# Attention and gated convolution: the last 64 keys' scores of two heads as two 64-row matmuls in place of one block matmul

## The chip, the core and the metric

One core of a Trainium2 chip runs the whole program. The metric is the device time of one execution in microseconds (us); three runs of the kernel before took 470.22, 471.49 and 474.07 us, and their median, 471.49, is the time before.

## The reference

The inputs are q, k and v of 4 batches, 8 heads, 576 positions and 64 elements, all float32. Rotary attention without a mask is followed by a feed-forward layer ("MoE" in the names) with a gate that looks at neighbouring positions:

```python
q_rot, k_rot = rotate(q), rotate(k)
scores = np.matmul(q_rot, k_rot.transpose(0, 1, 3, 2)) / np.sqrt(D)
scores = scores - np.max(scores, axis=-1, keepdims=True)
attn = np.exp(scores); attn = attn / (np.sum(attn, axis=-1, keepdims=True) + 1e-09)
x = np.matmul(attn, v)                        # then heads side by side: 4 x 576 x 512
h = np.maximum(x @ w_in, 0.0)                 # 512 -> 1024
conv_out[s] = sum(conv_w[k] * h[s + k - 1])   # k = 0, 1, 2, zero outside
out = (h * sigmoid(conv_out)) @ w_out         # 1024 -> 512
```

## The kernel before, in words

The 32 heads are taken two at a time, as 16 pairs p; head 0 of a pair lies on partitions 0 to 63 of the transposed queries and keys QT and KT, head 1 on 64 to 127. A pair has five steps s: four of 128 queries for each head, and a fifth (s = 4) with the last 64 queries of both heads together. Step m = 5p + s computes scores (`emit_S`), negated row maxima (DVE, L284), exponentials with row sums (ACT, L288), and in the next step transposes of the exponentials (`emit_T`, L336), which ACT evacuates into the tile `pt` (L216). The product of these with the values (`emit_E`, L415) comes a pair later, cut into four parts of 145 positions for the early pairs, and is evacuated as `xn` (L425).

The order of all engines' instructions is written out by hand. `plan[n]` holds the pieces of step n with a rank each; `at(n, rank, fn)` adds one, and the loop in `emit` takes them in the order of the ranks. Each engine executes its own instructions in that order, and semaphores between engines come from what is read and written.

The diff touches the steps in front of `WIDE = 26`, where there is no feed-forward work on PE yet (`"m" not in psum`). There a step n holds, by rank: 0, the transposes of step n - 1, head 0's eight and then head 1's eight (in a fifth step ten for both), and their evacuations on ACT; 0.19 to 0.5, pieces of the rotation on POOL (`rope_by_three`), the maxima (0.2) and exponentials (0.3) of step n, evacuations of what `spare` gave out a step before (0.35), the transposes of later queries and keys (`emit_TQ`, DVE, L249 and L252, 0.35), pieces of the weights' conversion from 64 to 32 bits (DVE, ACT, 0.4), and the scores of step n + 1 (0.5); 2, the remainder transpose (`emit_Trem`, L367); 4, the product part; 4.5 and later, DMAs and reciprocals.

A score tile `ps` has three banks of 512 columns, and two such tiles take turns. Head 0's scores are in columns 0 to 575, head 1's in 960 to 1535. The first 512 keys of a head are one 64-row matmul into a bank of its own (L276). The last 64 keys of both heads come from one 128-row matmul (L302) against `krem`, a block-diagonal 128 x 128 tile with head 0's last 64 keys in one corner and head 1's in the other; its output goes to columns 512 to 575 and 960 to 1023 of the middle bank:

```python
nc.tensor.matmul(
    out=ps[:, 512:1024].rearrange("p (g n) -> p g n", g=8)[:, 0:8:7, :],
    lhsT=qt[:, c], rhs=krem[p % 2], start=True, stop=True,
)
```

The corners of `krem` are filled by two 64 x 64 DVE transposes a pair (L256), or, for pair 0, by two DVE copies (L241); its zeros are set once. The columns between, 576 to 959, are handed out by `spare` to the remainder transpose and the product part of the same step, and evacuated by ACT in the next step behind the exponentials (`after`). The fifth step has no block matmul: its scores are 64 x 64 matmuls. A matmul in float32 stands in the trace as two records, each with a weight load (PEld).

Of the kernel before, what the change touches and what calls it, by code (L numbers as in the profile page):

```python
# [7 lines left out]
F32 = mybir.dt.float32  # L8
# [3 lines left out]
AF = mybir.ActivationFunctionType  # L12
# [8 lines left out]
def attention_moe_kernel(ctx, tc, q, k, v, w_in, conv_w, w_out, tab, tabx, out):  # L21
    nc = tc.nc
    B, H, S, D = q.shape
# [11 lines left out]
    STEPS = 5  # L35
    scale = float(D) ** -0.5
# [4 lines left out]
    psum = {}  # L41
# [25 lines left out]
    xT = keep.tile([128, NSLOT - NK, 2, XW], F32R, name="xT")  # L67
    wctx = ExitStack()
    wkeep = wctx.enter_context(tc.tile_pool(name="wk", bufs=1))
    krem = [wkeep.tile([128, 128], F32, name=f"kr_{s}") for s in range(2)]  # L70
    tabs = wkeep.tile([128, 480], F32, name="tabs")
    turnm = [tabs[:, 128 * i:128 * i + 128].rearrange("p (t i) -> p t i", t=4) for i in range(3)]
    turnr = [tabs[:, 384 + 32 * i:416 + 32 * i] for i in range(3)]
# [118 lines left out]
    def port(ins):  # L192
        late["v"] = ins
        return ins

    def gated(ins):
        tc.add_manual_dep(
            ins.ins, late["v"].ins.name, mybir.DependencyInfo(mybir.DependencyClass.Sync, mybir.DependencyReason.DATA), reason="port"
        )

    def rope_by_three(p, part):
        def mult(i):
# [9 lines left out]
    QT, KT = {}, {}  # L212

    def evac(eng, out, in_, sc=None):
        if eng == "A" or "m" not in psum:
            nc.scalar.activation(out=out, in_=in_, func=AF.Copy, scale=1.0 if sc is None else sc)  # L216
        elif sc is None:
            nc.vector.tensor_copy(out, in_)
        else:
            nc.vector.tensor_scalar(out=out, in0=in_, scalar1=sc, scalar2=None, op0=ALU.mult)  # L220
# [6 lines left out]
    def emit_TQ0(part, ps):  # L227
        qk_tiles(0)
        turned = [z.rearrange("p h d -> p (h d)") if part == "r" else z.rearrange("p t h d -> p t (h d)") for z in rot.pop(part)]
        for t in range(1 if part == "r" else 4):  # L230
            for i, z in enumerate(turned):
                nc.tensor.matmul(
                    out=ps[:, 0:128] if part == "r" else ps.rearrange("d (p t) -> d t p", t=4)[:, t, :],
                    lhsT=z if part == "r" else z[:, t, :], rhs=idf, start=(i == 0), stop=(i == 1),
                )
        if part == "r":
            evac("A", QT[0][:, 512:S], ps[:, 0:64])
            evac("A", KT[0][:, 576:640], ps[:, 64:128])
            for h in range(2):
                r = slice(64 * h, 64 * h + 64)  # L240
                nc.vector.tensor_copy(krem[0][r, r], ps[r, 64:128])  # L241
        else:
            evac("A", QT[0][:, 0:512] if part == "q" else KT[0][:, 64:576], ps)

    def emit_TQ(p, part):
        qk_tiles(p)
        x = raw.pop((p, part))[:, :, 0, :]
        if part == "q":
            nc.vector.transpose(out=QT[p].rearrange("p (c i) -> p c i", i=32), in_=x)  # L249
        else:  # L250
            kt = KT[p].rearrange("p (c i) -> p c i", i=32)
            nc.vector.transpose(out=kt[:, 2:20], in_=x)  # L252
            if p * STEPS < WIDE:
                for h in range(2):
                    r = slice(64 * h, 64 * h + 64)
                    nc.vector.transpose(out=krem[p % 2][r, r].rearrange("p (c i) -> p c i", i=32), in_=x[r, 16:18])  # L256
            if p * STEPS + STEPS > WIDE:
                nc.vector.transpose(out=kt[:, 0:2], in_=x[:, 16:18])

# [5 lines left out]
    def go(d, key):  # L265
        for fn in d.pop(key):
            fn()

    def emit_S(p, s):
        if s == 0:  # L270
            negm[p] = p2.tile([128, 9], F32, tag="negm", name="negm")
            sums[p] = p2.tile([128, 9], F32, tag="sums", name="sums")
        qt, kt = QT[p], KT[p]

        def mm(out, h, a, n, c):
            nc.tensor.matmul(  # L276
                out=out, lhsT=qt[64 * h:64 * h + 64, c], rhs=kt[64 * h:64 * h + 64, a:a + n], start=True, stop=True
            )

        def soft(sc, dst, col):  # L280
            nm, sm = negm[p][:, col:col + 1], sums[p][:, col:col + 1]
            if len(sc.shape) == 3:
                dst = dst.rearrange("p (j n) -> p j n", j=2)
            reds.setdefault((p, s), []).append(lambda: nc.vector.tensor_reduce(  # L284
                out=nm, in_=sc, axis=AX.XY if len(sc.shape) == 3 else AX.X, op=ALU.max, negate=True
            ))
            exps.setdefault((p, s), []).append(
                lambda: nc.scalar.activation(out=dst, in_=sc, func=AF.Exp, bias=nm, scale=1.0, accum_out=sm)  # L288
            )

        c = slice(128 * s, min(128 * s + 128, S))
        if s < 4:
            st = ST[p, s] = p1.tile([128, 2, S], F32, tag="st", name="st", bufs=3)
        else:
            st = STR[p] = strem[p % 2][:, 0:S]
        if "m" not in psum:
            ps = free["ps"] = psum["s"].tile([128, 1536], F32, tag="s", name="sp")
            free["at"] = 576
            if s < 4:
                mm(ps[:, 0:512], 0, 64, 512, c)  # L300
                mm(ps[:, 1024:1536], 1, 64, 512, c)
                nc.tensor.matmul(  # L302
                    out=ps[:, 512:1024].rearrange("p (g n) -> p g n", g=8)[:, 0:8:7, :],
                    lhsT=qt[:, c], rhs=krem[p % 2], start=True, stop=True,
                )
                for h in range(2):
                    soft(ps[:, 960 * h:960 * h + S], st[:, h, :], 5 * h + s)
            else:
                for h in range(2):
                    mm(ps[64 * h:64 * h + 64, 0:512], h, 64, 512, c)  # L310
                for h in range(2):
                    mm(ps[64 * h:64 * h + 64, 512:576], h, 576, 64, c)
                soft(ps[:, 0:S], st, 4)
        elif s < 4:
            pss_ = [psum["s"].tile([128, 2, 512], F32, tag="s", name="sp") for _ in range(2)]
            for j in range(2):
                for h in range(2):
                    mm(pss_[h][:, j, 0:HS], h, HS * j + 64 - 64 * h, HS, c)
            for h in range(2):
                soft(pss_[h][:, :, 0:HS], st[:, h, :], 5 * h + s)  # L320
        else:
            ps = psum["s"].tile([128, 2, 512], F32, tag="s", name="sp")
            for h, j in ((0, 0), (1, 1), (0, 1), (1, 0)):
                mm(ps[64 * h:64 * h + 64, j, 0:HS], h, HS * j + 64, HS, c)
            soft(ps[:, :, 0:HS], st, 4)
# [3 lines left out]
    def emit_T(p, s, h=None):  # L329
        if not h:  # L330
            tps[p] = [t_tile() for _ in range(2)]
        ps = tps[p]

        def turn(k, x, r):
            i = slice(64 * r, 64 * r + 64)
            nc.tensor.transpose(ps[r][:, 64 * k:64 * k + 64], x[i], idf[i, i])  # L336

        if s == 4:
            st = strem[p % 2]
            for t in range(4):  # L340
                for r in range(2):
                    turn(t, st[:, 128 * t:128 * t + 128], r)
            for r in range(2):
                turn(4, st[:, 512 - 64 * r:640 - 64 * r], r)
            evac("A", pt[:, 0:9:2, 512:S], ps[0][:, 0:320].rearrange("p (k c) -> p k c", k=5))
            evac("A", pt[:, 1:8:2, 512:S], ps[1][:, 0:256].rearrange("p (k c) -> p k c", k=4))
            evac("A", pt[64:128, 8, 512:S], ps[1][64:128, 256:320])
        else:
            for t in range(4):
                for r in range(2):  # L350
                    turn(2 * t + h, ST[p, s][:, h, 64 * h + 128 * t:64 * h + 128 * t + 128], r)
            def out():
                for r in range(2):
                    c = 128 * s + 64 * r
                    evac("A", pt[:, 0:8, c:c + 64], ps[r].rearrange("p (k c) -> p k c", k=8))

            if h and "m" in psum:
                at(late["n"], 2.2 if UNITS.get(late["n"]) == 2 else 1.6, out)
            elif h:
                out()  # L360
# [417 lines left out]
    def at(n, rank, fn):  # L778
        plan.setdefault(n, []).append((rank, len(plan.get(n, [])), fn))

    def emit():
        with tc.manual_schedule(engines=engines):
# [2 lines left out]
            load_w(0)  # L785
            load_cw()
            conv_cw(0)
            for x in rvc + krem + vrem + [x[:, S:S + 64] for x in strem]:
                nc.vector.memset(x, 0.0)
            for part in "qkr":  # L790
                rope0(part)
# [2 lines left out]
            nc.vector.tensor_copy(tabt[64:128], tabt[0:64])  # L794
            ps = psum["s"].tile([128, 1536], F32, tag="s", name="sp")
            for _ in range(10):
                nc.tensor.matmul(out=ps[:, 0:128], lhsT=krem[0], rhs=krem[1], start=True, stop=True)
            emit_TQ0("q", t_tile())
            wcv[0][0]()
            emit_TQ0("k", t_tile())  # L800
# [4 lines left out]
            at(0, 0.25, wcv[0][4])  # L805
            load(1, "q")
            load_w(1)
            emit_S(0, 0)
            load(1, "k")
            load_w(2)  # L810
# [158 lines left out]
```

## Time and profile before

| what | value |
|---|---|
| median of three runs | 471.49 us (470.22 to 474.07) |
| the profiled execution | 471.33 us, of which span 469.5 us |
| PE busy | 455.7 us, 97% of the span |
| DVE, ACT, POOL busy | 351.6, 327.4, 271.5 us |
| granted PE clock | 1.0 throughout |
| instructions | 12177 |

The span goes from the first to the last instruction; all times in the views are from its start. PE is TensorE's matmuls and transposes, PEld its weight loads, SP the queue that issues most DMAs. Busy PE time overlaps, since matmuls are pipelined: from start to start is what a matmul takes of the engine, and its length is more. A bracket in the timeline says how long the engine was idle before, and which instruction ended that.

### The profile page before, as it was taken

What the parts mean: (1) busy time and instruction counts of PE and PEld (TensorE: products, weight loads), DVE (VectorE), ACT (ScalarE), POOL (GpSimd) and SP (SyncE); (2) the same over time, 40 slices, a digit from 0 to 9 for tenths busy, and PEclk for the clock granted to TensorE, in tenths of its full rate; (3) what the DMA queues carried; (4) which work ended last, traced back from release to release, by engine and by line L of the source; (5) the groups of instructions that cost most, each with busy time, mean ns of one, the idle gap of its engine ahead of it and who ended that gap; (6) DMA issues with size and microseconds to landing.
All of it is one profiled execution on the core that took longest, in us unless ns stands there. A gap on an engine that the chain in (4) does not pass through costs nothing.

```text
span 469.5 us, 12177 instructions
## 1 busy us (share of the span) xinstructions
PE 455.7 (97%) x4555; PEld 356.8 (76%) x4555; DVE 351.6 (75%) x648; ACT 327.4 (70%) x940; POOL 271.5 (58%) x403
## 2 busy tenths in 40 slices
PE   8789999989999999999999999999999999999997
PEld 7456656657666778788797979788787878999886
DVE  6898998868999898667686877866755748368921
ACT  3878879978897878868696868778686844245400
POOL 0944466587799696988849493929320334133510
PEclk9999999999999999999999999999999999999999
DMA  9979695552480716034161716142010000100011
GB/s 233 266 174 208 153 199 125 147 133 53 119 188 12 128 38 137 27 77 75 38 140 41 138 38 139 39 112 64 28 50 28 24 28 0 46 23 24 0 68 45
DMA packets 103630, 42.32 MB, mean 90 GB/s; under 512 B 94524, under 2 KB 97876, under 8 KB 103572
## 3 DMA queue, kind: packets, MB, share of 16 engines
q1 hardware_dynamic: 103120, 41.20, 38.0%
q8 instruction: 36, 0.59, 0.6%
q10 hardware_dynamic: 452, 0.35, 0.2%
q14 instruction: 22, 0.18, 0.1%
HBM read 36.74 MB, written 4.79 MB: 88 GB/s over the span
## 4 chain that ended last, share of the span: by engine, by line
PE 80%; ACT 8%; DVE 6%; DMA 2%; POOL 1%; SPq 1%; issue 1%; ACTq 0%; DVEq 0%; POOLq 0%
PE sp L276 13%; PE pm L415 12%; PE pm L594 11%; PE mt L574 11%; PE pm L482 10%; PE mt L482 7%; PE tp L336 7%; PE pm L472 5%; PE sp L415 3%; ACT st L288 3%; ACT pt L216 2%; DVE negm L284 2%; DMA rk<-k 1%; DMA idf<-tab 1%; POOL rk L187 1%; DVE wt L630 1%
## 5 line engine op out<-in xcount | busy, mean ns | idle before, releaser
L284 DVE TENSOR_REDUCE negm<-sp 128x1 f32<-128x576 f32 x144 | 102.7, 750 | 24.3 <-PE sp L276 17.9
L288 ACT ACTIVATE st<-sp,negm 128x576 f32<-128x576 f32 x128 | 93.8, 741 | 25.0 <-DVE negm L284 21.0
L276 PE MATMUL sp<-kT,qT 64*128 64x288 f32 (+4 forms) x556 | 94.3, 449 | 0.5 <-ACT pt L216 0.3
L216 ACT ACTIVATE pt<-tp 128x512 f32<-128x512 f32 (+3 forms) x176 | 84.5, 533 | 6.6 <-PE tp L336 6.1
L503 DVE SCALAR_TENSOR_TENSOR c<-rr,cw,c 128x288 f32<-128x288 f32 x128 | 80.5, 629 | 4.3
L521 POOL TENSOR_TENSOR gm<-c,gm 128x288 fp32r<-128x288 f32 (+4 forms) x72 | 46.4, 649 | 49.8 <-ACT gm L520 48.4
L276 PEld LDWEIGHTS sp<-kT,qT 64*128 64x128 f32 (+1 forms) x556 | 44.5, 174 | 22.5 <-issue 9.0
L336 PEld LDWEIGHTS tp<-idf,st 64*128 64x128 f32 x1024 | 41.1, 138 | 20.2 <-ACT st L288 8.4
L336 PE MATMUL tp<-idf,st 64*128 64x64 f32 x1024 | 46.8, 226 | 4.9 <-ACT st L288 4.6
L187 POOL TENSOR_TENSOR rq<-rq,tabt 128x192 f32<-128x192 f32 x60 | 40.3, 703 | 17.4 <-DMA rq<-q 13.1
L415 PE MATMUL pm<-pt,vm 128*64 128x290 f32 x368 | 49.8, 411 | 0.4 <-ACT pt L216 0.4
L594 PE MATMUL pm<-wouth,gm 64*128 64x256 f32 x512 | 49.6, 284 | 0.0
L512 DVE SCALAR_TENSOR_TENSOR c<-c,rr 128x288 f32<-128x288 f32 x64 | 36.6, 592 | 9.8 <-ACT c L509 9.7
L187 POOL TENSOR_TENSOR rk<-rk,tabt 128x192 f32<-128x192 f32 x60 | 39.8, 696 | 3.0 <-DMA rk<-k 3.0
L594 PEld LDWEIGHTS pm<-wouth,gm 64*128 64x128 f32 x512 | 41.4, 185 | 0.0
L501 DVE TENSOR_SCALAR c<-rr,cw 128x288 f32<-128x288 f32 x56 | 24.1, 430 | 22.7 <-ACT rr L493 22.4
L415 PEld LDWEIGHTS pm<-pt,vm 128*64 128x64 f32 x368 | 25.5, 136 | 17.9 <-ACT pt L216 1.0
L440 POOL TENSOR_TENSOR xT<-xn,xT 128x290 fp32r<-128x290 f32 x18 | 15.7, 876 | 36.9 <-ACT xT L436 36.9
L482 PE MATMUL pm<-xT,wh 128*128 128x290 f32 x176 | 37.0, 302 | 0.0
L594 PE MATMUL pm<-woutl,gm 64*128 64x256 f32 x256 | 36.8, 278 | 0.0
L509 ACT ACTIVATE c<-c 128x288 f32<-128x288 f32 x64 | 28.5, 445 | 11.4 <-DVE c L503 11.4
L472 PE MATMUL pm<-xr,wr 128*128 128x290 f32 x128 | 34.5, 417 | 0.0
(141 smaller groups left out, 988.1 us busy)
## 6 DMA issues: line engine op xcount, KB each, us to landing
rq<-q SPq DMA_DIRECT2D x60, 144.0 KB
rk<-k SPq DMA_DIRECT2D x60, 144.0 KB
w<-moe_w_in SPq DMA_DIRECT2D x8, 512.0 KB
vm<-v SPq DMA_DIRECT2D x32, 128.0 KB
rb<-rd SPq DMA_DIRECT2D x16, 144.0 KB
out<-oh SPq DMA_DIRECT2D x18, 128.0 KB
rb<-rd SPq DMA_DIRECT2D x16, 128.0 KB
w<-moe_w_out SPq DMA_DIRECT2D x4, 512.0 KB
```

The lines of the kernel that those rows point to most:

```text
L187: nc.gpsimd.tensor_tensor(out=y, in0=y, in1=tabt[:, a:a + 3], op=ALU.mult)
L216: nc.scalar.activation(out=out, in_=in_, func=AF.Copy, scale=1.0 if sc is None else sc)
L276: nc.tensor.matmul(out=out, lhsT=qt[64 * h:64 * h + 64, c], rhs=kt[64 * h:64 * h + 64, a:a + n], start=True, stop=True)
L284: reds.setdefault((p, s), []).append(lambda: nc.vector.tensor_reduce(out=nm, in_=sc, axis=AX.XY if len(sc.shape) == 3 else AX.X, op=ALU.ma ...
L288: lambda: nc.scalar.activation(out=dst, in_=sc, func=AF.Exp, bias=nm, scale=1.0, accum_out=sm)
L336: nc.tensor.transpose(ps[r][:, 64 * k:64 * k + 64], x[i], idf[i, i])
L415: nc.tensor.matmul(out=xp[64 * h:64 * h + 64, :], lhsT=vmain[p][:, h, i, :] if i < 4 else vrem[p % 2][:, h, :], rhs=pt[:, 2 * i + h if i < ...
L472: nc.tensor.matmul(out=ps[:, 0:XW], lhsT=raws[kk, half][:, gs], rhs=xraw[kk, j], start=(kk == 0), stop=(kk == NK - 1))
L482: nc.tensor.matmul(out=ps[:, 0:XW], lhsT=w, rhs=x_at(xs, e), start=(i == 0), stop=(i == n - 1))
L503: nc.vector.scalar_tensor_tensor(out=c, in0=r[:, j + e:j + e + HS], scalar=cw[:, 8 * e + f:8 * e + f + 1], in1=c, op0=ALU.mult, op1=ALU.add,)
L574: nc.tensor.matmul(out=ops[tt][:, 0:width], lhsT=g_tile(tt, f, e), rhs=w[:, f, cols], start=(f == 0 and i == 0), stop=(f == NF - 1 and i = ...
L594: nc.tensor.matmul(out=ps[r][:, 0:256], lhsT=g_tile(tt, f, e)[rows], rhs=w[rows, f, cols], start=(f == 0 and i == 0), stop=(f == NF - 1 an ...
```

## The change

The block matmul, `krem` and all that fills it go. For steps s < 4 in front of `WIDE`, each head's last 64 keys are a 64-row matmul of 64 columns against KT. Head 0's (`emit_rest0`) is issued in step n for step n + 1 between head 0's and head 1's transposes, or in front of the ten transposes of a fifth step; the score tile is taken at that place (`begun`). Head 1's (`emit_rest1`) is issued at rank 4.2 of the same step, behind the product part, with a wait for ACT's first evacuation of that step's transposes (`late["turned"]`). For steps 0 and 1 both come with the scores, and a one-column ACT copy (`dot`) stands for the evacuation. The warm-up matmuls take a tile `zero`.

```diff
-    krem = [wkeep.tile([128, 128], F32, name=f"kr_{s}") for s in range(2)]
+    zero = wkeep.tile([128, 128], F32, name="zero")
+    dot = wkeep.tile([128, 1], F32, name="dot")
...
+    def sync_on(ins, prior, why):
+        tc.add_manual_dep(
+            ins.ins, prior.ins.name, mybir.DependencyInfo(mybir.DependencyClass.Sync, mybir.DependencyReason.DATA), reason=why
+        )
...
             evac("A", KT[0][:, 576:640], ps[:, 64:128])
-            for h in range(2):
-                r = slice(64 * h, 64 * h + 64)
-                nc.vector.tensor_copy(krem[0][r, r], ps[r, 64:128])
...
             nc.vector.transpose(out=kt[:, 2:20], in_=x)
-            if p * STEPS < WIDE:
-                for h in range(2):
-                    r = slice(64 * h, 64 * h + 64)
-                    nc.vector.transpose(out=krem[p % 2][r, r].rearrange("p (c i) -> p c i", i=32), in_=x[r, 16:18])
...
+    def by_head(p):
+        qt, kt = QT[p], KT[p]
+
+        def mm(out, h, a, n, c):
+            return nc.tensor.matmul(
+                out=out, lhsT=qt[64 * h:64 * h + 64, c], rhs=kt[64 * h:64 * h + 64, a:a + n], start=True, stop=True
+            )
+
+        return mm
+
+    begun = {}
+
+    def emit_rest0(p, s):
+        ps = begun[p, s] = psum["s"].tile([128, 1536], F32, tag="s", name="sp")
+        if s < 4:
+            by_head(p)(ps[:, 512:576], 0, 576, 64, slice(128 * s, 128 * s + 128))
+
+    def emit_rest1(p, s, ps):
+        sync_on(by_head(p)(ps[:, 960:1024], 1, 576, 64, slice(128 * s, 128 * s + 128)), late["turned"], "bank")
...
-            ps = free["ps"] = psum["s"].tile([128, 1536], F32, tag="s", name="sp")
+            ps = free["ps"] = begun.pop((p, s))
...
-                nc.tensor.matmul(
-                    out=ps[:, 512:1024].rearrange("p (g n) -> p g n", g=8)[:, 0:8:7, :],
-                    lhsT=qt[:, c], rhs=krem[p % 2], start=True, stop=True,
-                )
+                if p == 0 and s < 2:
+                    emit_rest1(p, s, ps)
+                else:
+                    at(late["n"], 4.2, lambda: emit_rest1(p, s, ps))
...
+        if (h or s == 4) and late["n"] + 1 < WIDE:
+            emit_rest0(*divmod(late["n"] + 1, STEPS))
         if s == 4:
...
-            evac("A", pt[:, 0:9:2, 512:S], ps[0][:, 0:320].rearrange("p (k c) -> p k c", k=5))
+            late["turned"] = evac("A", pt[:, 0:9:2, 512:S], ps[0][:, 0:320].rearrange("p (k c) -> p k c", k=5))
...
-                    evac("A", pt[:, 0:8, c:c + 64], ps[r].rearrange("p (k c) -> p k c", k=8))
+                    ins = evac("A", pt[:, 0:8, c:c + 64], ps[r].rearrange("p (k c) -> p k c", k=8))
+                    if not r:
+                        late["turned"] = ins
...
-            for x in rvc + krem + vrem + [x[:, S:S + 64] for x in strem]:
+            for x in rvc + [zero] + vrem + [x[:, S:S + 64] for x in strem]:
...
-                nc.tensor.matmul(out=ps[:, 0:128], lhsT=krem[0], rhs=krem[1], start=True, stop=True)
+                nc.tensor.matmul(out=ps[:, 0:128], lhsT=zero, rhs=zero, start=True, stop=True)
...
+            emit_rest0(0, 0)
+            emit_rest0(0, 1)
+            late["turned"] = nc.scalar.activation(out=dot, in_=begun[0, 1][:, 512:513], func=AF.Copy)
             emit_S(0, 0)
```

## Rows read from the trace of the kernel before

**Rows 1.** Busy time by stretch: five engines, granted clock, DMA share

```profile
10.00:95.00 85.00, 77.66 (x880) 48.73 (x878) 77.96 (x137) 72.84 (x194) 50.31 (x48) 1.00 0.80 184
95.00:225.00 130.00, 128.18 (x1294) 95.22 (x1291) 108.71 (x186) 106.86 (x309) 110.76 (x170) 1.00 0.40 89
```

**Rows 2.** Chain that ended last, 10 to 100 us: start, length, what

```profile
17.57 4.20 POOL rk L187 x6
...
24.36 0.24 DVE kr L256
...
31.66 0.46 PE tp L336 x8
...
45.84 0.42 PE sp L302 x2
...
49.20 0.42 PE sp L302 x2
...
66.93 1.52 DVE wt L630
...
83.35 0.42 PE sp L302 x2
```

**Rows 3.** Instructions of L302 and L256: duration ns min/median/max, first and last start

```profile
L302 PEld LDWEIGHTS sp<-kr,qT x42: 186/188/189, 11.6 to 93.7; 128*128 128x128 f32 x42
L302 PE MATMUL sp<-kr,qT x42: 275/326/377, 11.6 to 93.8; 128*128 128x128 f32 x42
L256 DVE STREAM_TRANSPOSE kr<-rk x10: 194/219/243, 24.1 to 91.0; 64x64 f32<-64x64 f32 x10
```

**Rows 4.** Timeline, one step: start, length, instruction, tiles, form [idle before]

```profile
65.90 0.49 PE L302 MATMUL sp<-kr,qT 128*128 128x128 f32 x2
...
66.22 0.27 PE L367 MATMUL sp<-idf,st 128*128 128x128 f32 x1
...
66.43 1.21 PE L415 MATMUL sp<-pt,vm 128*64 128x145 f32 x16
...
67.81 0.58 PEld L336 LDWEIGHTS tp<-idf,st 64*128 64x128 f32 x16 [0.20 <-ACT xn L425]
67.81 0.71 PE L336 MATMUL tp<-idf,st 64*128 64x64 f32 x16
...
68.36 1.08 PE L276 MATMUL sp<-kT,qT 64*128 64x512 f32 x4
```

**Rows 5.** Page, part 5, weight loads of L336: count | busy, mean ns | idle before

```profile
L336 PEld LDWEIGHTS tp<-idf,st 64*128 64x128 f32 x1024 | 41.1, 138 | 20.2 <-ACT st L288 8.4
```

**Rows 6.** Timeline, a step whose scores have no block matmul

```profile
73.31 0.33 PE L367 MATMUL sp<-idf,st 128*128 128x128 f32 x1
...
73.56 1.21 PE L415 MATMUL sp<-pt,vm 128*64 128x145 f32 x16
```

**Rows 7.** Timeline, transposes and what ACT does just before them

```profile
64.34 0.20 ACT L288 ACTIVATION_READ_ACCUMULATOR st<-sp,negm 128x1 f32 x1
...
64.60 0.46 PE L336 MATMUL tp<-idf,st 64*128 64x64 f32 x8 [0.26 <-ACT st L288]
...
75.58 0.35 ACT L425 ACTIVATE xn<-sp 128x145 f32<-128x145 f32 x1
...
75.64 0.46 PE L336 MATMUL tp<-idf,st 64*128 64x64 f32 x8 [0.23 <-ACT st L288]
...
81.82 0.27 ACT L216 ACTIVATE pt<-sp 128x128 f32<-128x128 f32 x1
...
81.98 0.46 PE L336 MATMUL tp<-idf,st 64*128 64x64 f32 x8 [0.26 <-ACT st L288]
```

**Rows 8.** Timeline, the maxima of a step and the exponential after them

```profile
38.46 1.42 DVE L284 TENSOR_REDUCE negm<-sp 128x1 f32<-128x576 f32 x2 [1.05 <-PE sp L415]
...
40.06 0.74 ACT L288 ACTIVATE st<-sp,negm 128x576 f32<-128x576 f32 x1
```

**Rows 9.** Waits of ACT from 14 to 94 us: total us, times, longest

```profile
ACT pt L216 <- PE tp L336: 5.4, 14, 0.8
```

More of the change, by code (lines that the diff above doesn't have):

```diff
@@ L194, in port @@
         return ins
+    def sync_on(ins, prior, why):
+        tc.add_manual_dep(
+            ins.ins, prior.ins.name, mybir.DependencyInfo(mybir.DependencyClass.Sync, mybir.DependencyReason.DATA), reason=why
+        )
     def gated(ins):
-        tc.add_manual_dep(
-            ins.ins, late["v"].ins.name, mybir.DependencyInfo(mybir.DependencyClass.Sync, mybir.DependencyReason.DATA), reason="port"
-        )
+        sync_on(ins, late["v"], "port")
     def rope_by_three(p, part):
@@ L215, in evac @@
         if eng == "A" or "m" not in psum:
-            nc.scalar.activation(out=out, in_=in_, func=AF.Copy, scale=1.0 if sc is None else sc)
+            return nc.scalar.activation(out=out, in_=in_, func=AF.Copy, scale=1.0 if sc is None else sc)
         elif sc is None:
@@ L272, in emit_S @@
             sums[p] = p2.tile([128, 9], F32, tag="sums", name="sums")
-        qt, kt = QT[p], KT[p]
-        def mm(out, h, a, n, c):
-            nc.tensor.matmul(
-                out=out, lhsT=qt[64 * h:64 * h + 64, c], rhs=kt[64 * h:64 * h + 64, a:a + n], start=True, stop=True
-            )
+        mm = by_head(p)
         def soft(sc, dst, col):
@@ L301, in emit_S @@
                 mm(ps[:, 1024:1536], 1, 64, 512, c)
-                nc.tensor.matmul(
-                    out=ps[:, 512:1024].rearrange("p (g n) -> p g n", g=8)[:, 0:8:7, :],
-                    lhsT=qt[:, c], rhs=krem[p % 2], start=True, stop=True,
-                )
+                if p == 0 and s < 2:
+                    emit_rest1(p, s, ps)
+                else:
+                    at(late["n"], 4.2, lambda: emit_rest1(p, s, ps))
                 for h in range(2):
```

## The prediction

> **What bounds the kernel now.** I read the windows by stage first. From 95 us on TensorE (PE) is busy for 99% (the row to 225 us stands for it); before that, in the stage the change touches, for 91%, with VectorE (DVE) at 92% and ScalarE (ACT) at 86% [rows 1]. So a microsecond won or lost in front of 95 us should reach the end whole, and in front of it three engines share the limit. What lies where is read from the chain of waits. Up to 23 us it is the load of the second pair's keys and their rotation on GpSimd (POOL); to 31 us DVE; then PE; around 40 us ACT; from 44 to 58 us PE; to 70 us DVE; to 82 us ACT; then PE again; one row stands for most of these [rows 2]. The block matmul of L302 stands on that chain seven times, always in a PE stretch, six times as at 49.20 and 83.35, and once, at 45.84, where no remainder transpose (L367) follows it [rows 2].
>
> **A step.** Step n has on PE: transposes of step n-1 (L336, head 0's eight, head 1's eight), scores of n+1 (L276), the block matmul (L302), the remainder transpose (L367), the product (L415). ACT goes: evacuation of the transposes, two exponentials of step n, then the evacuations of the score tile's spare columns (L216 `pt<-sp`, L425 `xn`), which L367 and L415 wrote a step before. Score tiles have two buffers, so the tile of n+1 is the one whose spare columns ACT has just evacuated.
>
> **What goes.** 21 block matmuls, 42 records [rows 3]. In a step with L367 and product, from the block's start to the product's it is 66.43 - 65.90 = 0.53 us [rows 4]; where the block is missing, from L367 to the product 73.56 - 73.31 = 0.25 [rows 6]. So the block costs 0.28 us of PE's time there, 0.42 where no L367 follows [rows 2]. DVE loses ten small transposes of 0.22 us, two a pair of heads [rows 3]; the first pair is on the chain, of which 24.36 is the second one [rows 2], and gives back 0.45 us. The others lie ahead of reductions that wait for PE or in ACT's stretches: nothing.
>
> **What comes.** Two 64-row, 64-column matmuls a step, two passes each. No such matmul is in the trace. Nearest are L336's transposes, of the same rows, columns and height: 16 in 68.36 - 67.81 = 0.55 us, 0.07 a pair on the two row halves [rows 4]. The new ones use one half, so a pass costs a pair's slot: 2 x 0.07 = 0.14 us each. Bounds: nothing, if the other half's transposes or the change of tile shape before the next L336 hide it; at most the whole block's start-to-next, 66.22 - 65.90 = 0.32 us [rows 4], which streams twice the columns. I take 0.14. A step then pays 0.28 and saves 0.28: zero for six of the seven steps on PE's path, and -0.14 for the seventh.
>
> A rule speaks against 0.14. The Trainium skill ("TensorE: Matmul & The Clock Gate", section "Part 3: Packing small matmuls — row/col tiling") says that weight loads overlap running matmuls only where the row group differs. By that rule each pass would pay its own load, and the sum would be that of the second rival below. The trace does not agree here: 16 loads stand in 0.58 us on two row halves [rows 4], though one takes 138 ns [rows 5], so that eight on one half, each waiting for the half to be free, would take 1.1 us for the loads alone.
>
> **The new wait, head 0's.** Its matmul writes into the reused tile, and stands between head 0's and head 1's transposes (in front of all ten after a fifth step). It must wait until ACT has evacuated that tile's spare columns; queued behind it are the transposes, and ACT's own next work waits for these. Before, they waited for the exponential alone, and the scores behind them for the evacuation. The delay is the evacuation's end plus 0.06 us (an exponential's last record to the transposes it frees: 64.54 to 64.60 [rows 7]) less the transposes' start. Where only the remainder's evacuation is left, at 81.98, that is 81.82 + 0.27 + 0.06 - 81.98 = 0.17 us, and as much at 31.66 [rows 2]; where `xn` follows, at 75.64, 75.58 + 0.35 + 0.06 - 75.64 = 0.35 [rows 7], and as much in front of the ten transposes of the fifth steps at 44.36 and 78.00. In steps where PE comes late and waits for nothing, as at 67.81 [rows 4], the evacuation is over by the time head 0's transposes are done: nothing. The one at 64.60 and three like it lie where DVE sets the end: nothing. At 78.00 I take 0.2 us as covered, since ACT has a weight operation to do there before it needs the transposes. Sum on the path: 2 x 0.17 + 2 x 0.35 + 0.15 = 1.19 us. At 75.64 and 78.00 the path runs through ACT, not through the scores, so there the matmul's own 0.14 comes on top without the saving: +0.28.
>
> **The new wait, head 1's.** It follows the product and waits for ACT's first transpose evacuation of that step, which by then has ended in every step I followed. The maxima (L284) of both heads wait already for the product: DVE stood idle for 1.05 us until it ended [rows 8]. They will wait for this matmul too, some 0.25 us more. From the maxima's end to the exponential there are 40.06 - (38.46 + 1.42) = 0.18 us of slack [rows 8], and the score work in front of it is 0.28 shorter: nothing. Without that cover it would be 0.25 in about six steps, 1.5 us. The transposes behind it start at the change of shape they paid already.
>
> **The start.** Head 0's matmuls of steps 0 and 1, the one-column ACT copy and the missing DVE copies change the first maxima by some tenths; the chain there is the load and POOL, which none of it touches [rows 2]: nothing. No DMA is moved, and the SP and POOL queues keep their order; with the small transposes gone DVE's releases for POOL come no later.
>
> **Sum.** -0.45 (DVE) - 0.14 (PE) + 1.19 + 0.28 (waits) = +0.88 us. The profiled execution took 471.33 us (span 469.5), 0.16 below the median of 471.49; 471.33 + 0.88 = 472.2, and by the median 472.4. I say **472.3 us**.
>
> **Rivals.**
> 1. *The small matmuls hide.* They cost PE nothing, and the evacuations end earlier because PE's steps do. Then the seven blocks are won: 6 x 0.28 + 0.42 = 2.1, and 0.45 of DVE: 471.33 - 2.55 = 468.8 us; with half of the waits left, 469.4. For it: one row half is idle beside each. Against: five transposes on the path already start at the instant ACT lets them [rows 7].
> 2. *The weight loads do not overlap*, on the slower side. Each pass pays a load of 0.19 us (L302's [rows 3]): 0.38 a matmul, 0.76 a step against 0.28 saved, +0.48 in seven steps = 3.4, and 2 x 0.24 more at 75.64 and 78.00, 3.8 in all. With the 0.88: 471.33 + 4.7 = 476.1 us. It decides once a pass takes over 0.07 us where PE has no slack. Against: the transposes' pitch.
> 3. *The waits do not matter*, since in the longer step ACT has caught up, while the matmuls cost what I say: -0.59 us, 470.7.
>
> **How the numbers follow.** Forecast 0.52 (471.3 to 474), rival 1 0.16, rival 3 0.19, rival 2 0.09, something unforeseen 0.04. The bounds of the matmuls (0 and 0.32 on seven steps: -2 and +2.5 us) and the uncovered 1.5 us of head 1 carry the range from rival 1's end to short of rival 2: **469.4 to 475.4 us**. Runs of before lie between 470.22 and 474.07, so about 1%, 4.7 us, is what can be told from no change. Rival 2's upper half and part of the unforeseen are slower than that: 0.08; more than 1% faster needs more than all seven blocks and the DVE work: 0.05; within 1%: 0.87.
>
> **What would show it.** Right: ACT's waits for L336 (5.4 us from 14 to 94 us, 14 times [rows 9]) grow by about 1 us and more; head 1's transposes start some 0.2 us after `xn`'s end where they were at the exponential's; in the step at 67.81 PE's step stays at 3.5 us; the maxima start 0.2 to 0.3 us after the product. Wrong in the price, if a 64-row pass takes other than 0.07 us of PE's time; wrong in the mechanism, if head 0's matmul starts before ACT's evacuation, or if the chain between 31 and 95 us is PE's throughout. If the stretch up to 95 us changes little and the time moves, the cause is behind it, and nothing above speaks of that.

## The result, and the profile after

The changed kernel took **476.33 us** (median of 7 runs, 474.99 to 477.80), the kernel before on the same chip 472.56 us (7 runs, 470.22 to 474.07): a ratio of **1.0073, interval 1.0053 to 1.0092**. The forecast was 472.3 us with a range to 475.4, so the time lies above the range. The profiled execution took 477.8 us (span 476.0).

Busy time by stretch of the changed kernel, in the columns of [rows 1]:

```profile
10.00:95.00 85.00, 78.77 (x869) 52.33 (x869) 69.66 (x118) 69.56 (x183) 48.81 (x46) 0.94 0.82 177
95.00:225.00 130.00, 127.62 (x1254) 93.82 (x1250) 108.78 (x186) 106.53 (x305) 106.28 (x161) 1.00 0.43 94
```

Up to 95 us PE is busy for 93% now, DVE only for 82% (92% in [rows 1]); this execution also granted PE less clock there (0.94 for 1.00), to which I come at the end. ACT's waits for the transposes, 14 to 94 us, the row that answers to [rows 9]:

```profile
ACT pt L220 <- PE tp L348: 10.0, 19, 1.0
```

It was 5.4 us in 14 waits; the forecast's sign was a growth of about 1 us and more, and it is 4.6. L302 and L256 [rows 3] are gone; L270 is now the line of the scores and of the small matmuls, L348 of the transposes. To see where the time goes, the start of each step's first exponential was read from the timelines of every run. The table has the differences in us; 0 to 6 means from that of step 0 to that of step 6, step 8 means from that of step 8 to that of step 9, and the change's steps end with 25.

| kernel | 0 to 6 | 6 to 25 | 25 to 28 | 28 to 34 | 34 to the end |
|---|---|---|---|---|---|
| before, first profile | 19.52 | 63.75 | 14.49 | 27.63 | 330.56 |
| before_again | 21.09 | 63.59 | 14.50 | 27.66 | 330.24 |
| after, first profile | 20.96 | 65.95 | 14.61 | 28.61 | 330.49 |
| after_again | 19.91 | 66.15 | 14.92 | 28.15 | 330.59 |
| evac_first | 21.02 | 66.04 | 14.74 | 28.11 | 331.14 |
| late0b | 19.07 | 63.80 | 14.62 | 28.22 | 330.61 |
| after_kr | 20.39 | 65.88 | 14.49 | 28.20 | 330.65 |
| late0b_kr | 20.38 | 63.48 | 14.48 | 28.40 | 330.74 |
| before_nokr | 19.34 | 63.10 | 14.63 | 27.61 | 330.59 |
| after_layout | 20.28 | 65.94 | 14.87 | 27.97 | 330.89 |

The rows below after_again are the experiments. Steps 0 to 6 differ by up to 1.6 us between executions of one kernel, and tell nothing. Steps 6 to 25 do: 2.2 to 2.6 us longer with the change. Behind them come 0.1 to 0.4 and then 0.5 to 1.0 us more in the two executions of the changed kernel, in steps whose instructions the change does not touch.

**What a step shows.** In the kernel before, steps that ACT sets take as little as 3.07 us (steps 15 and 20) and those that PE sets 3.47. With the change, in after_again, three places are longer: steps 8 to 10 by 0.6 us, 18 to 20 by 1.4 and 23 by 0.2. Steps 11 to 17, which hold the stretch that DVE ends in the kernel before, take the same as a whole: 24.36 us, and 24.43 before. (Steps 6 and 7 add 0.2 here, but they also differ from one execution to the next.) Step 20, which took 3.07 us and now takes 3.47, in after_again; first ACT, then PE (start, length, instruction):

```profile
84.67 0.73 ACT L300 ACTIVATE st<-sp,negm 128x576 f32<-128x576 f32 x1
85.30 0.20 ACT L300 ACTIVATION_READ_ACCUMULATOR st<-sp,negm 128x1 f32 x1
85.39 0.28 ACT L220 ACTIVATE pt<-sp 128x128 f32<-128x128 f32 x1
86.44 0.60 ACT L220 ACTIVATE pt<-tp 128x512 f32<-128x512 f32 x1 [0.77 <-PE tp L348]
```

```profile
84.50 0.43 PE L270 MATMUL sp<-kT,qT 64*128 64x64 f32 x2
84.83 0.46 PE L348 MATMUL tp<-idf,st 64*128 64x64 f32 x8
85.72 0.32 PE L270 MATMUL sp<-kT,qT 64*128 64x64 f32 x1 [0.43 <-ACT pt L220]
85.73 0.33 PE L348 MATMUL tp<-idf,st 64*128 64x64 f32 x2
85.88 0.27 PE L270 MATMUL sp<-kT,qT 64*128 64x64 f32 x1
85.90 0.43 PE L348 MATMUL tp<-idf,st 64*128 64x64 f32 x5
```

Head 1's exponential is out at 85.50. Head 0's matmul waits for the spare evacuation, starts at 85.72, and the transposes behind it release ACT at 86.44, 0.94 us after the exponential. Without the matmul in front, in late0b (a run described below), it is 81.62 to 82.17, 0.55 us:

```profile
81.42 0.20 ACT L300 ACTIVATION_READ_ACCUMULATOR st<-sp,negm 128x1 f32 x1
81.51 0.28 ACT L220 ACTIVATE pt<-sp 128x128 f32<-128x128 f32 x1
82.17 1.09 ACT L220 ACTIVATE pt<-tp 128x512 f32<-128x512 f32 x2 [0.39 <-PE tp L348]
```

```profile
80.95 0.46 PE L348 MATMUL tp<-idf,st 64*128 64x64 f32 x8
81.67 0.47 PE L348 MATMUL tp<-idf,st 64*128 64x64 f32 x8 [0.26 <-ACT st L300]
```

The difference, 0.39 us, is the step's growth. Of it 0.17 is the wait (85.72 instead of 85.50 + 0.05) and 0.22 the matmul itself (0.72 from its start to the evacuation, for 82.17 - 81.67 = 0.50 from the transposes' start). The chain of waits of after_again runs right through it (start, length, what):

```profile
83.94 1.55 ACT st L300 x4
85.50 0.18 ACT pt L220
...
85.72 0.28 PE sp L270
...
86.34 0.98 PE sp L270 x4
87.31 0.26 PE sp L383
87.57 1.39 PE sp L431 x20
88.96 0.21 PE sp L270
```

In step 23 nothing waits in front of the matmul, since PE comes late, and it is longer by 0.24 us all the same: the evacuation's wait for the transposes grows from 0.53 to 0.77 us. The kernel before, then after_again:

```profile
92.08 0.71 PE L336 MATMUL tp<-idf,st 64*128 64x64 f32 x16
...
92.82 0.60 ACT L216 ACTIVATE pt<-tp 128x512 f32<-128x512 f32 x1 [0.53 <-PE tp L336]
```

```profile
96.00 0.46 PE L348 MATMUL tp<-idf,st 64*128 64x64 f32 x8
96.32 0.32 PE L270 MATMUL sp<-kT,qT 64*128 64x64 f32 x1
...
97.04 0.60 ACT L220 ACTIVATE pt<-tp 128x512 f32<-128x512 f32 x1 [0.77 <-PE tp L348]
```

### The profile page after: what moved, and what is told of

Same layout as the page of the kernel before. It is cut to its first block, busy times and chain, and to the rows that moved or that the text cites. A ratio compares the mean times of both kernels' runs of the same rounds, so it can differ in the third digit from the quotient of the medians.

```text
span 476.0 us, 12249 instructions
## 1 busy us (share of the span) xinstructions
PE 461.3 (97%) x4597; PEld 363.0 (76%) x4597; DVE 348.1 (73%) x635; ACT 328.4 (69%) x941; POOL 272.1 (57%) x403
## 4 chain that ended last, share of the span: by engine, by line
PE 82%; ACT 10%; DVE 4%; DMA 2%; issue 1%; DVEq 0%; ACTq 0%
PE sp L270 16%; PE pm L610 11%; PE pm L431 11%; PE mt L590 11%; PE pm L498 10%; PE tp L348 7%; PE mt L498 7%; PE pm L488 4%; PE sp L431 4%; ACT pt L220 3%; ACT st L300 3%; DMA w<-moe_w_in 1%; DVE c L519 1%; DVE negm L296 1%; DMA rq<-q 1%; PE sp L383 1%
## 5 line engine op out<-in xcount | busy, mean ns | idle before, releaser
L270 PE MATMUL sp<-kT,qT 64*128 64x288 f32 (+5 forms) x640 | 116.0, 438 | 5.1 <-ACT xn L441 2.4
L270 PEld LDWEIGHTS sp<-kT,qT 64*128 64x128 f32 (+1 forms) x640 | 59.8, 178 | 33.0 <-issue 12.5
L348 PEld LDWEIGHTS tp<-idf,st 64*128 64x128 f32 x1024 | 47.5, 143 | 12.6 <-issue 2.3
L348 PE MATMUL tp<-idf,st 64*128 64x64 f32 x1024 | 52.8, 230 | 1.7 <-ACT st L300 1.4
L528 DVE SCALAR_TENSOR_TENSOR c<-c,rr 128x288 f32<-128x288 f32 x64 | 38.1, 616 | 9.8 <-ACT c L525 9.8
```

The source lines that it names most:

```text
L270: return nc.tensor.matmul(out=out, lhsT=qt[64 * h:64 * h + 64, c], rhs=kt[64 * h:64 * h + 64, a:a + n], start=True, stop=True)
```

## The experiments

The edits are shown shortened, "..." marking what is left out.

**Both kernels again.** before_again and after_again are the two kernels unchanged.

> The kernel before, unchanged, timed against itself: 472.6 us, ratio 1.00 within 0.004. Its second trace shows how much of the two traces' distance is the execution and not the change: the scores of step 0 began at 10.50 us before and at 12.20 us after. If the start is chance, this trace may begin its scores anywhere from 10.4 to 12.2 us; if the change makes it, this one is near 10.5 again. Granted clock 1.0 throughout by the theory that only the changed kernel loses its clock.

> The changed kernel, unchanged: 476.3 us, ratio 1.007. Theory of the wait: from step 6 on the distance to the kernel before grows by 2.0 to 2.5 us up to step 25, 0.6 us of it in each fifth step, whatever the clock does. Rival, the clock: the granted clock is under 1.0 somewhere between 15 and 30 us, and where it is 1.0 throughout, the time is within 2 us of the kernel before. Rival, the price: the steps that wait for nothing are over 3.6 us long instead of 3.47.

Measured: 472.51 us, 0.9993 (0.9976 to 1.0009), and 475.62 us, 1.006 (1.0039 to 1.0081); the kernel before had a median of 473.15 in 18 runs here. The slowdown repeats, in an execution whose clock was 1.0 throughout, so the clock is not its cause. before_again lost clock too (0.79 from 25 to 30 us), and its scores of step 0 began at 11.73 us, for 10.50 in the first profile and 12.20 in that of the changed kernel: neither belongs to the change. The 471.49 us that the forecast started from was a median of three.

**Head 0's matmul behind all transposes, first try: late0.**

```
-        if (h or s == 4) and late["n"] + 1 < WIDE: emit_rest0(...)   # between the transposes
+        def rest0(): ...   # called behind head 1's transposes
+            at(late["n"], 0.21, lambda: late.update(turned=nc.vector.tensor_copy(dot, begun_at[m][:, 512:513])))
```

> Head 0's small matmul is issued behind head 1's transposes (behind all ten of a fifth step), straight in front of the scores; head 1's waits for a one-column DVE copy of it that is issued behind the maxima. So the transposes wait for the exponentials alone again, as before the change, while both small matmuls stay. Theory of the wait: 2 to 3 us less than the changed kernel, 473.3 to 474.3 us, ratio 1.000 to 1.004. Rival, the price of the small matmuls: no change, 476 us. Rival, the clock of the start: no change, 476 us.

Measured: 488.93 us, 1.0331 (1.0291 to 1.0372). The one-column copy that was to order head 1's matmul behind head 0's brought a wait of its own. It stands on DVE behind the maxima, and the large scores, which write the same tile, waited for it (the waits of late0, 10 to 115 us: us, times, longest):

```profile
PE sp L270 <- DVE dot L356: 16.0, 19, 1.7
```

The expected 473.3 to 474.3 us did not come. It says nothing on the theory, only what a wait in front of the scores costs: 16.0 us in 19 steps.

**Spare evacuations ahead of the exponentials: evac_first.**

```
-            at(late["n"] + 1, 0.35, fn)
+            at(late["n"] + 1, 0.25, fn)
```

> The changed kernel, but ACT evacuates the spare columns of a score tile in front of the step's exponentials and not behind them (rank 0.25 for 0.35). Head 0's matmul then waits for no more than the exponential that head 1's transposes wait for anyway. The exponentials themselves come up to 0.5 us later, and with them all transposes. Theory of the wait: the idle time of PE in front of head 0's matmuls falls from 0.7 to under 0.5 us in the fifth steps, and the time is 474 to 476.5 us, as the late exponentials give part back. Rival, the price, and rival, the clock: no gain, 476 to 478 us.

Measured: 477.19 us, 1.0088 (1.0064 to 1.0111); 66.04 us from step 6 to 25, as in the changed kernel. The evacuation that head 0's matmul waits for has now long ended, and the same step looks so:

```profile
83.97 0.28 ACT L220 ACTIVATE pt<-sp 128x128 f32<-128x128 f32 x1
...
85.48 0.21 ACT L300 ACTIVATION_READ_ACCUMULATOR st<-sp,negm 128x1 f32 x1
86.46 1.09 ACT L220 ACTIVATE pt<-tp 128x512 f32<-128x512 f32 x2 [0.77 <-PE tp L348]
```

From the exponential to ACT's release it is 86.46 - 85.69 = 0.77 instead of 0.94, so the wait's 0.17 is gone; but the evacuation's 0.17 (83.97 to 84.14) stands in front of the exponentials, on the same path through ACT. The step is not shorter. The matmul's 0.22 stays. The expected 474 to 476.5 us did not come, and PE's idle time in front of head 0's matmuls still reaches 0.7 us; the time is the one that both rivals gave, though the clock is ruled out by after_again.

**The move alone: late0b.** Head 0's matmul behind head 1's transposes, ordered by an evacuation that is there anyway.

```
+            mm = rest0()                 # behind the transposes
             def out():
                 for r in range(2):
                     ins = evac("A", pt[:, 0:8, c:c + 64], ...)
-                    if not r: late["turned"] = ins
+                    if r: sync_on(ins, mm, "bank"); late["turned"] = ins
```

> The changed kernel with one move: head 0's 64-column matmul is issued behind head 1's transposes (behind the ten transposes of a fifth step), and the second evacuation of the transposes is made to wait for it, so that head 1's small matmul still comes after it. No instruction is added; the transposes no longer stand behind a wait for the spare evacuation. Theory (the wait in the middle of the transposes, paid in every step whose evacuation waits for TensorE): the stretch between steps 5 and 25 gives back some 2.0 of its 2.3 to 2.8 us, ACT's waits for the transposes fall from 9.0 to about 5 us, and the ratio to the kernel before falls from 1.006 to about 1.002; what is left is the 1.0 us behind step 27. Rival (it is the price of the small matmuls themselves, not the place where one waits): the stretch stays at 66.0 to 66.2 us from step 6 to step 25 and the ratio at 1.006. Second rival (the wait only moves to the scores that stand behind it): the scores' waits grow by what the transposes' lose, and the ratio stays within 0.002 of 1.006.

Measured: 473.65 us, 1.0029 (1.0012 to 1.0047). Steps 6 to 25 take 63.80 us, those of the kernel before: all of the 2.2 to 2.6 us come back. ACT's waits from 30 to 101 us, in before_again, after_again and late0b:

```profile
ACT pt L216 <- PE tp L336: 4.3, 12, 0.8
ACT st L288 <- DVE negm L284: 3.8, 7, 1.4
```

```profile
ACT pt L220 <- PE tp L348: 9.0, 18, 0.8
ACT st L300 <- DVE negm L296: 0.5, 1, 0.5
```

```profile
ACT pt L220 <- PE tp L348: 4.8, 13, 0.5
ACT st L300 <- DVE negm L296: 4.0, 6, 1.3
```

The transposes' waits fall to their old size, and DVE's come back with them: in the changed kernel DVE was ahead only because ACT and PE had become slower. The theory of the place holds, and both rivals fall: the small matmuls are all still there. The move takes out of the place both the wait and the matmul's own time; the two are told apart only by step 20 and step 23 above. Of the 1.2 us that are left between the medians, 0.7 stand behind step 25 (14.62 and 28.22 us in the table).

**The two small DVE transposes: after_kr, before_nokr, late0b_kr.**

```
+                    nc.vector.transpose(out=dead[r, ...], in_=x[r, 16:18])     # after_kr, and late0b_kr on top of late0b
-                    nc.vector.transpose(out=krem[p % 2][r, r], in_=x[r, 16:18])  # before_nokr
```

> The changed kernel with the two small DVE transposes of each pair of heads put back where they stood, into a tile that nothing reads: 0.45 us of DVE work per pair again, no other change. Theory (the two transposes were a spacer on DVE: without them the next query load leaves about 0.5 us earlier, GpSimd starts its products earlier, and DVE's conversions of the last weights, which run beside them, take 1.1 instead of 0.7 us in front of ScalarE): the jumps of some 0.4 us at step 28 and 0.5 us at step 34 are gone, the time from step 25 to the end falls from 373.6 to about 372.5 us, the stretch before it stays, and the ratio falls from 1.006 to about 1.004. Rival (DVE work is DVE work: putting it back costs): 0 to +0.45 us on top of the changed kernel, ratio 1.006 to 1.007, the jumps stay.

> The kernel before without the two small DVE transposes of pairs 1 to 5 that lay out the block matmul's right side: that matmul then reads what lies in its tile, so the last 64 keys' scores of these pairs are not those of the reference, and nothing else is left out. It is one part of the change alone. Theory (the transposes were a spacer in front of the query loads of the mixed steps): no gain up to step 25 (plus or minus 0.3 us), the same jumps of 0.4 to 0.5 us at steps 28 and 34, the time from step 25 to the end 373.2 to 373.6 instead of 372.5 us, ratio 1.001 to 1.002. Rival, the prediction's own term: 0.45 us of DVE time comes out, ratio 0.999, no jumps.

> Both edits on the changed kernel: head 0's small matmul behind head 1's transposes, and the two small DVE transposes put back as dead work. If both theories hold and their parts add up, 2.0 and 1.0 us come out of the 2.9 us by which the changed kernel is longer, and the ratio to the kernel before is 0.999 to 1.001. If only the place of the wait counts, 1.002; if only the spacer counts, 1.004; if neither, 1.006.

Measured: after_kr 475.79 us, 1.007 (1.005 to 1.0091); before_nokr 470.93, 0.998 (0.9959 to 1.0001); late0b_kr 473.80, 1.0024 (1.0007 to 1.004). In the old order the transposes do cost: 63.10 us from step 6 to 25 against 63.59 and 63.75, all of it in steps 14 to 16 (9.74 us against 10.38 and 10.42). This is one execution, and the medians' ratio has 1 in its interval; the expectation for before_nokr missed, and its rival, the prediction's own term, is nearer. In the changed kernel they cost nothing (65.88 us with them, 65.95 and 66.15 without). What late0b costs from step 6 to 25 depends on them: without them 63.80 for 63.10 us (before_nokr), 0.7 more, with them 63.48 (late0b_kr) for 63.59 and 63.75, nothing. Why the two pairs differ stays open. late0b_kr's ratio is the one expected if only the place counts.

The transposes also move later steps, but little: step 27 takes 4.18 us in the four kernels of the table that have them, and 4.31 to 4.61 in the others. There, DVE's conversion of the last weights meets GpSimd's products; the changed kernel, then after_kr:

```profile
113.81 2.85 POOL L188 TENSOR_TENSOR rq<-rq,tabt 128x192 f32<-128x192 f32 x3 [4.33 <-DVE c L519]
114.13 1.08 DVE L651 SCALAR_TENSOR_TENSOR room<-room 128x512 int32<-128x512 int32 x1
```

```profile
113.64 2.53 POOL L189 TENSOR_TENSOR rq<-rq,tabt 128x192 f32<-128x192 f32 x3 [4.23 <-DVE c L524]
113.49 0.69 DVE L656 SCALAR_TENSOR_TENSOR room<-room 128x512 int32<-128x512 int32 x1
```

Without the transposes DVE turns the queries 0.2 to 0.8 us earlier before step 27, the next query load leaves earlier, GpSimd starts first, and DVE's operation takes 1.08 instead of 0.69 us. It is the order of the starts that goes with the length in all 14 profiles: DVE's operation starts 1.52 or 1.53 us after the step's first exponential where GpSimd does not hold up what is in front of it; where GpSimd starts at 1.57 us or later the step takes 4.18 us, at 1.43 us or before it 4.31 or more. The transposes are not all that moves this start: late0 lacks them and starts at 1.57 (4.18 us), and before_dma, which has DMAs in their place, issues its load when before_again does and starts at 1.38 instead of 1.70 (4.31 us). The Trainium skill ("SBUF — State Buffer", section "SBUF: two separate sides") says that an operation of DVE with two inputs in SBUF and one of GpSimd that reads SBUF share a pair of ports, which the one that starts first holds for its whole length. The order of the starts here agrees; the length agrees less, since in the changed kernel DVE's operation is 0.39 us longer where GpSimd's first product had 0.53 us left. The expected fall of after_kr to 1.004 did not come: the larger jump, at step 33, stayed.

**Step 33: after_layout.**

```
-    dot = wkeep.tile([128, 1], F32, name="dot")
+    dot = wkeep.tile([128, 128], F32, name="dot")[:, 0:1]
```

> The changed kernel with the one-column tile that begins the order of the small matmuls given the room of one of the two removed tiles, so that every tile behind it lies in SBUF where it lay before; no instruction changes. It is one look at the 0.5 us by which step 33 is longer in each of the six kernels of the changed order and in none of the three of the order before (4.84 to 5.11 against 4.37 to 4.43 us). Theory (the place of the later tiles makes the query load land earlier): step 33 takes 4.4 us. Rival (it is the time at which the load meets the other transfers and DVE): 4.8 to 5.1 us again.

Measured: 476.01 us in one execution, and step 33 takes 4.73 us; it is not the place of the tiles. What goes with the length is when GpSimd's products start. Where they start 0.27 us or more after the step's first exponential, the step takes 4.37 to 4.50 us (five kernels of the old order); where they start at 0.23 us or before it, 4.73 to 5.15 us (nine of the new order, late0b the 0.23). The two sets are also the two orders, so the start is a coincidence that fits, not a cause that is shown. Why the load lands earlier there, though it is issued at about the same point, stays open.

**The price of a small matmul: rest1_x4.**

```
-        sync_on(by_head(p)(ps[:, 960:1024], 1, 576, 64, ...), late["turned"], "bank")
+        for _ in range(4):
+            sync_on(by_head(p)(ps[:, 960:1024], 1, 576, 64, ...), late["turned"], "bank")
```

> The changed kernel with head 1's small matmul issued four times, into the same place: three more 64-column matmuls behind the product of each of the 20 steps that have one, no other change. It measures the price of one where nothing waits. If a small matmul costs TensorE 0.12 to 0.14 us, as the steps that wait for nothing lead one to think (3.49 us with two small ones against 3.47 us with the block), these steps become 0.36 to 0.42 us longer, and the kernel 3.5 to 8 us (20 steps, some of which wait for ScalarE and hide a part): ratio 1.014 to 1.023. Rival, the prediction's first rival (a weight load and 64 columns hide beside the neighbours): less than 0.1 us a step, ratio 1.006 to 1.010.

Measured: 484.58 us, 1.026 (1.0219 to 1.0302). That is above the expected range. The steps that PE sets take 4.12 instead of 3.47 us: three more matmuls cost 0.65, **0.22 each**, not 0.14. Its passes on one row half start 0.11 us apart; two of them, with the weight load of the second between:

```profile
57.37 0.27 PE L270 MATMUL sp<-kT,qT 64*128 64x64 f32 x1
57.43 0.19 PEld L270 LDWEIGHTS sp<-kT,qT 64*128 64x128 f32 x1
57.48 0.27 PE L270 MATMUL sp<-kT,qT 64*128 64x64 f32 x1
```

By the rule of the Trainium skill that the prediction weighed ("TensorE: Matmul & The Clock Gate", "Part 3: Packing small matmuls — row/col tiling") weight loads overlap running matmuls only where the row group differs. The price measured here lies between the forecast's 0.14 and the 0.38 that rival 2 made of that rule. In the records the load of 0.19 us, of the same rows, starts while the pass in front is still running, but ends of matmuls are modelled, so they don't decide how much of it is hidden. In the changed kernel each small matmul has transposes of the other half beside it, and the steps that PE sets stay at 3.46 to 3.49 us: there the two together cost the block's 0.28 and 0.02 at most.

**The old order without the DVE transposes: before_dma, before_dma2.**

```
-                    nc.vector.transpose(out=krem[p % 2][r, r]..., in_=x[r, 16:18])
+                    nc.sync.dma_start(out=krem[p % 2][r, r], in_=KT[p][r, 576:640])   # before_dma2: pairs 2 to 5 only
```

> The kernel before with its block matmul, whose right side for pairs 1 to 5 comes from the transposed keys by two 64x64 DMAs of SP's queue in place of the two small DVE transposes. The run without those transposes was 0.65 us shorter from step 6 to step 25 and 0.14 us longer from step 25 to step 28. Theory (0.45 us of DVE work stood on the path in the stretch of steps 14 to 17, and nowhere else): 63.1 us from step 6 to step 25 instead of 63.6 to 63.75, ratio 0.998 to 0.999. Rival (the two DMAs stand in SP's queue in front of the next loads, wait there for the transposed keys and make GpSimd's products late): 63.6 us or more, ratio 1.000 to 1.003.

> As the kernel before with DMAs for the block matmul's right side, but for pair 1 the two small DVE transposes stay, since there the matmul waited up to 4.5 us for the DMA beside the weights' loads; pairs 2 to 5 take the DMAs. Theory (the DVE transposes cost up to 0.6 us in steps 14 to 17, and a DMA that lands in time costs nothing): 63.1 to 63.5 us from step 6 to step 25 against 63.6 to 63.75, no waits of the block matmul for the DMA, ratio 0.998 to 1.000. Rival (the loads behind the two DMAs on SP's queue come late): 1.001 to 1.003.

Measured: 473.94 us, 1.0033 (1.0005 to 1.006), and 471.83 us, 1.0001 (0.9981 to 1.002). The block matmul waits for these DMAs (PE's waits, of before_dma from 10 to 101 us and of before_dma2 from 30 to 101):

```profile
PE sp L302 <- DMA kr<-kT: 5.2, 3, 3.7
```

```profile
PE sp L305 <- DMA kr<-kT: 2.5, 2, 2.0
```

From step 6 to step 25 they take 63.46 and 65.22 us, and 63.1 and 63.1 to 63.5 were expected. before_dma2 was expected not to wait, and did. So the 0.6 us that before_nokr shows were not had this way, and no version here that leaves nothing out beats the kernel before.

## Why the prediction was wrong

- **The step that failed: the price of head 0's matmul, "there the matmul's own 0.14 comes on top without the saving: +0.28".** The new wait was right in mechanism, place and size: head 0's matmul starts 0.05 us after the evacuation's end, and the delays are those forecast (table below). What the prediction had wrong is the matmul's own time. It counted 0.14 us at two places, and elsewhere set it off against the block. But the block stood behind the transposes, and this matmul stands in front of them. So ACT gets the transposes later by the matmul's own time in every step in which it waits for them, also where the matmul itself waits for nothing (steps 8 and 23), while what the block saves comes only behind them. It is 0.21 to 0.24 us in six steps between 6 and 25: 1.32 us in all, where the forecast had 0.28. From after_again and the first trace of before, in us:

| step (place in the prediction) | wait, forecast | wait, measured | matmul, forecast | matmul, measured | step longer by |
|---|---|---|---|---|---|
| 8 | 0 | 0 | 0 | 0.24 | 0.24 |
| 9 (44.36) | 0.35 | 0.36 | 0 | 0.21 | 0.31 |
| 18 (75.64) | 0.35 | 0.38 | 0.14 | 0.21 | 0.60 |
| 19 (78.00) | 0.15 | 0.20 | 0.14 | 0.21 | 0.38 |
| 20 (81.98) | 0.17 | 0.17 | 0 | 0.22 | 0.40 |
| 23 | 0 | 0 | 0 | 0.23 | 0.24 |

  The wait is how much later head 0's matmul starts in its step than the transposes did (in step 19, 0.36 less 0.16 that ACT's weight operation covers); the matmul is what the evacuation comes later beyond that. In step 9, 0.26 us of the sum does not show, since ACT waited for DVE there before. The fifth wait, at 31.66, is step 5, in front of the stretch: 3.07 us in the first trace of before, 3.46 in after_again. Steps 11 to 17 gain and lose in turn and come to nothing in all, as the prediction said of the steps there that DVE ends.
- **Its price per pass.** The prediction named a sign for this: a 64-row pass that takes other than 0.07 us. It is some 0.11, in front of head 1's transposes as in a row on one half. Moving head 0's matmul off the place (late0b) gives the 2.2 to 2.6 us back, so it is the place that costs; that the time is rival 2's, 476.1 us, is a coincidence.
- **The price on PE's path**, 0.28 against 0.28, was right: steps that PE sets, 3.47 us, are 0.00 to 0.02 us longer.
- **The DVE term, -0.45.** "The others ... nothing" was wrong for the old order, where the small transposes of the later pairs cost 0.5 to 0.65 us (before_nokr, one execution), but their removal is worth nothing in the changed kernel. Whether the first pair gave its 0.45 back can't be read, since steps 0 to 6 vary by more.
- **Head 1's wait** cost nothing that the waits show, as forecast: ACT's waits for the maxima fell from 3.8 to 0.5 us. **"DVE's releases for POOL come no later"** was right, but earlier was not asked for. Step 27 is 0.1 to 0.4 us longer where GpSimd's products start ahead of DVE's operation, and putting the transposes back takes that away; step 33 is 0.3 to 0.7 us longer, and what moved the load there is open. The prediction had no term behind 95 us.
- **The base.** 472.56 us in 7 runs and 471.70 to 473.15 in the medians of the later comparisons, for 471.49 and 471.33: some 1 us of the miss belongs to no step.

Added up from the traces: 2.2 to 2.6 us from step 6 to 25, 0.1 to 0.4 at step 27, 0.5 to 1.0 behind it, 2.8 to 4.0 in all. The medians differ by 3.8 and, in the repeat, 2.5 us.

## What to carry to other kernels

Before you put an instruction between a producer and a consumer on another engine, count two things in every step where that consumer waits: what the instruction waits for, and its own time. The own time is paid also where it waits for nothing. What is saved behind that point does not repay it, even if the engine's own sum of work stays the same. And where a small operation on a shared tile needs an order, hang it on an instruction that exists: a marker of one column became a wait in front of the next step's scores.

## What the runs showed of the chip that was not expected

PE's granted clock fell to half, or near it, for some microseconds between 15 and 30 us in some executions of both kernels and not in others: after, before_again and after_again, 20 to 25 us, in the columns of [rows 1]:

```profile
20.00:25.00 5.00, 4.97 (x38) 2.98 (x36) 3.64 (x6) 3.49 (x10) 5.00 (x9) 0.50 1.07 281
```

```profile
20.00:25.00 5.00, 3.61 (x32) 1.88 (x30) 3.59 (x7) 3.81 (x10) 5.00 (x9) 0.87 1.08 269
```

```profile
20.00:25.00 5.00, 4.13 (x38) 2.25 (x40) 3.85 (x7) 4.04 (x10) 5.00 (x10) 1.00 1.03 275
```

0.50 is the lower of its two levels, 1.2 of 2.4 GHz. PE had been idle in part before: from 15 to 20 us it was busy for 3.46 of 5 us in after (0.83 granted), for 3.11 in before_again and 3.21 in after_again (both 1.00), so its busy time there does not tell the three apart. Steps 0 to 6 took 20.96 and 21.09 us in after and before_again, and 19.91 and 19.52 in after_again and the first trace of before, whose clock stayed at 1.0: the lost clock goes with part of the 1.6 us by which they vary, and single executions don't rank these kernels.
